# Per-column maxima sent to DRAM as rows, fewer transfers, another PSUM pool for the next keys and values, and a quad every 15.5 units in a planned attention-and-mixer kernel

## The chip, the cores and the metric

One core of a Trainium2 chip runs the whole program; the metric is the device time of one execution in microseconds (us). The engines named here are TensorE (PE, with its weight loads as PEld), VectorE (DVE), ScalarE (ACT), GpSimd (POOL) and SyncE (SP). Transfers are issued by SP, a few by ACT, and each of the two has a queue of its own that takes its instructions in order; 16 DMA engines carry the data.

## The reference

For each of 8 batches and 8 heads there are 576 positions, 64 channels and 32 memory slots. The softmax of `phi` runs over the positions, and so needs the maximum of each of the 32 columns; the sums it weights are the memory's keys and values. Queries attend to these 32 slots, and the result goes through a mixer over tokens and one over channels.

```python
a = np.exp(phi - np.max(phi, axis=2, keepdims=True))      # over the 576 positions
a = a / (np.sum(a, axis=2, keepdims=True) + 1e-09)
k_m = np.einsum('bhsm,bhsd->bhmd', a, k);  v_m = np.einsum('bhsm,bhsd->bhmd', a, v)
scores = scale * np.matmul(q, k_m.transpose(0, 1, 3, 2))
attn = softmax(scores)                                    # over the 32 slots
x = np.matmul(attn, v_m)                                  # then (batch, position, head*channel)
u = x + (np.maximum(x^T @ w_tok1, 0) @ w_tok2)^T          # token mixer
out = u + np.maximum(u @ w_ch1, 0) @ w_ch2                # channel mixer, d_ch = 1536
```

## The kernel before

Work comes in two kinds. A **quad** (b, Q) is four heads of one batch: 16 in all. A **chunk** c is 512 rows of the channel mixer: 9 in all. The program has three stages. In the first, weights are unpacked, the quads (0,0) to (1,1) run, and chunk 0's products start. In the second, which is the one that the change touches, the twelve quads (2,0) to (7,1) of the list `late` run beside chunks 1 and 2. In the third, chunks 3 to 8 run in pairs, with fewer products (their operands are sums of quarters).

The order of all instructions of the second stage is laid down ahead of time by `plan` (line 961): a list scheduler with a duration for each step, one timeline for each engine, a rank for each step (`PERIOD * n` spaces the ranks of the quads), and rooms (buffers) that a step takes. It yields one list; each engine then runs its part of that list strictly in order, with semaphores where data or buffers ask for them. The planner's durations set the order alone. On the chip an instruction that waits holds up all behind it on its engine.

A late quad goes so: `load_turned` (616) brings phi of four heads, one (head, column) on each partition; `phi_max` (620) reduces each partition to one number on DVE; `max_out` (624) writes these 128 numbers to 512 bytes of DRAM, one four-byte word from each partition; `max_in` (628) reads the 512 bytes back to all 128 partitions. POOL subtracts them from phi in its other layout (631), ACT takes the exponential (444), and PE forms keys and values in one PSUM bank `kvp` (`get_kv`, 450). Then come `scales`, `spread_T`, `turn_T`, `get_kb` for the keys and `spread_v`, `v_high`, `v_low` for the values; `scores` (490); the softmax on DVE and ACT, with `ul` (195) and the like between; `rows_out` (544) and `rows_in` (680) turn the result by way of DRAM in pieces of 128 bytes; `nat`, `A`, `R`, `attend` and `u` are the token mixer. A chunk's products `cp` (146) are evicted by ACT (`hh`, 115) and DVE (`hl`, 118) and go into `acc` (169). PSUM has two banks with the tag `at`, two with `ch` and four accumulators; in this kernel every bank of a quad is an `at`, and `ch` belongs to the chunks.

`Sums` writes to DRAM, beside all this, the weight sums that stage three reads back (`load_unit`); `store_u` puts a quad's result in DRAM for the chunks 3 to 8.

Of the kernel before, what the change touches and what calls it, by code (L numbers as in the profile page):

```python
# [10 lines left out]
F32 = mybir.dt.float32  # L11
# [4 lines left out]
ALU = mybir.AluOpType  # L16
AX = mybir.AxisListType
# [3 lines left out]
P = 128  # L21
# [7 lines left out]
def kernel(  # L29
# [312 lines left out]
    class Sums:  # L342
# [5 lines left out]

        def unit(s, j):
            return s.to[:, j].rearrange("p (o x a n) -> p o x a n", o=2, x=2, a=2)  # L350

        def words(s):
# [54 lines left out]
    def load_unit(eng=nc.scalar):  # L407
        if not unit_queue:
            return
        z, p, j = unit_queue.pop(0)  # L410
        t = sb.tile([P, 1024], F32R, tag="c1", name=f"unit{z}{p}{j}", bufs=NF)
        units[z, p, j] = t.rearrange("p (o x a n) -> p o x a n", o=2, x=2, a=2)
        m = 512 if j == 3 else 1024
        eng.dma_start(out=f32(t)[:, :m], in_=sums[p].to[:, j, :m])

# [9 lines left out]
    class Quad:  # L425
# [114 lines left out]
        def rows_out(s):  # L540
            s.rows = dram.tile([S, 4 * M], F32, name="rows" + s.n, tag="rows", bufs=2)
            for i in range(4):
                eng = nc.scalar if i % 2 and (s.b, s.Q) == (4, 0) else nc.sync
                eng.dma_start(
                    out=s.rows[:, i * M : (i + 1) * M].rearrange("(a t) m -> t a m", t=32),
                    in_=s.S[32 * i : 32 * i + 32],
                )
# [60 lines left out]
    class LateQuad(Quad):  # L608


        def __init__(s, b, Q):
            s.b, s.Q, s.n, s.up = b, Q, f"_{b}_{Q}", {}

        def load_turned(s):
# [25 lines left out]
        def get_kv(s):  # L640
            s.step_kv()

# [4 lines left out]

        def vb_room(s):
            s.vb = side[0][:, 640:896]

        def spread_v(s):
            s.vb_room()
# [109 lines left out]

        def spill(s, db):
# [196 lines left out]

    def plan(rank, ways, slow=None, slack=0.0):

# [8 lines left out]
        needs = {z: len(z.after) for z in steps}  # L971
        free, taken, landed, port = {}, {}, 0.0, 0.0
# [26 lines left out]
        while left:  # L999
# [32 lines left out]
    LATE = 2  # L1032
    MARGIN = 0.85
    RANKS = (
# [567 lines left out]
    class ThirdBatchQuad(SecondQuad):  # L1602
# [6 lines left out]

        def spread_v(s):  # L1610
            LateQuad.vb_room(s)
            s.spread_values(s.vb, s.kvp[:, D : 2 * D])

        def get_kv(s):
            s.kvp = bank([P, CW], "kvp" + s.n)
            s.mm_kv()
# [174 lines left out]
    def room(tag, n=1):  # L1791
        return Room((tag, n))
# [15 lines left out]
    def todo_at(t, *args, **kw):  # L1808
        z = step(*args, **kw)
        key[z] = -t  # L1810
        return z
# [36 lines left out]
    u_done = []  # L1848
    PERIOD, START, behind = 12.0, 3.0, []
    for n, qd in enumerate(late):  # L1850
        t0 = START + PERIOD * n

        def do(t, *args, **kw):
            return todo_at(t0 + t, *args, **kw)

        bk, kb, vh, vl, vb, T = room("at", 2), room("kb"), room("vh", 2), room("vl", 2), room("side vb"), room("vb") if n else room("pr", 2)
        per = room("ps", 3)
        if n:
            phi_room, kv_r, q_r = room("phi", 2), room("kv"), room("qT")
            m, r, turned = room("ps", 3), room("pr", 2), room("al", 2)  # L1860
# [4 lines left out]
            z = do(-26, "SP", 0.8, qd.load_phi, begin, take=[phi_room], move=0.9)  # L1865
            y = do(-22, "SP", 0.5, qd.max_in, y, z, take=[r])
            z = do(-16, *PHI_SUB(qd), y, z, use=[phi_room, r], port=True)
            e = do(-13, "ACT", 0.8, qd.phi_only_exp, z, use=[phi_room])
            l = do(-20, "SP", 0.5, qd.load_kv, begin, take=[kv_r], move=3.5)
            lq = do(-12, "SP", 0.6, qd.load_q, begin, take=[q_r], move=1.6)  # L1870
            kvuse, after = [phi_room, kv_r], [e, l]
        else:
            kvuse, after, q_r, lq = [pt2, kv2], [begin], q2, begin
# [4 lines left out]
        else:  # L1878
            y = do(-8, "DVE", 0.35, qd.spread_T, z, take=[T], use=[bk])
        v = do(-7, "DVE", 0.48, qd.spread_v, z, y, sided, take=[vb], use=[bk, side_room, per])  # L1880
        y = do(-7, "PE", 0.12, qd.turn_T, y, use=[bk, T])
        y = do(-6, "ACT", 0.3, qd.get_kb, y, v, take=[kb], use=[bk])
        v = vhigh = do(-5, "ACT", 0.42, qd.v_high, v, take=[vh], use=[vb, side_room])
# [34 lines left out]
        for hf in range(2):  # L1918
# [5 lines left out]
            for db, bk in enumerate(bks):  # L1924
# [14 lines left out]
                wrote[db].append(h)  # L1939
        for db in range(2):  # L1940
            if qd.spill(db):
                z_ = do(25 + db, "SP", 0.5 * len(qd.spill(db)), lambda qd=qd, db=db: qd.store_u(db), *wrote[db], use=[stage[db], side_room], move=0.8)
                z_.lands = True
                u_done.append((qd, z_))

# [52 lines left out]
    for p, x in enumerate(sums):  # L1998
        t0 = SUMS_AT[p]
        w = room("wide", 5)  # L2000
        z = todo_at(t0, "SP", 2.6, x.store_rest, begin, use=c1_rooms[p], move=1.0)
        z.not_before = t0
# [15 lines left out]
            190 + 40 * t, "SP", 0.5, lambda t=t: pr.load(t),  # L2018
            *(z for qd, z in u_done if any(c == pr.c + t for db in range(2) for c, _, _ in qd.spill(db))),
            added[1, NKK - 1], take=[uv[t]], move=2.9,  # L2020
# [427 lines left out]
```

## Time and profile before

| What | Value |
|---|---|
| Runs shown | 784.11, 794.3 and 1462.78 us, median 794.3 us |
| The profiled execution | 790.09 us, span 788.0 us from first to last instruction |
| TensorE granted clock, mean over the span | 0.969 |
| PE busy | 733.8 us, 93% |
| PEld, DVE, ACT, POOL busy | 76%, 64%, 44%, 11% |
| DMA | 101239 packets, 41024 of them under 512 bytes; 196 GB/s over the span |

The profile cuts the span into 40 slices of 19.7 us and gives the busy share of each engine in tenths. Below it names groups of instructions with their mean duration, the idle time ahead of them and what ended it, the transfers with the time from issue to landing, and the chain of work that ended last. The clock granted to TensorE stands beside PE: 1.00 is 2.4 GHz, 0.50 is 1.2 GHz.

### The profile page before, as it was taken

To read this page: it belongs to the slowest core of one execution; us is meant where nothing else is said; L and a number is where in the kernel's file an instruction comes from. 1 tells how busy PE (TensorE), PEld (TensorE's weight loads), DVE (VectorE), ACT (ScalarE), POOL (GpSimd) and SP (SyncE) were. 2 spreads that over 40 slices of the span, in tenths; PEclk is the share of its full clock that TensorE was granted. 3 is DMA by queue.
4 is the path that set the end of the run, shared out by engine and by line. 5 is a ranking of instruction groups with operands and counts; after the bars stand their busy time and mean duration, and the time that the engine had idled before them with its cause. 6 is when DMAs were issued, how large, how long until landed. Compare 5 with 4: busy or idle time off the path is not lost.

```text
span 788.0 us, 11573 instructions
## 1 busy us (share of the span) xinstructions
PE 733.8 (93%) x4371; PEld 596.1 (76%) x4371; DVE 505.2 (64%) x830; ACT 348.6 (44%) x627; POOL 89.7 (11%) x82
## 2 busy tenths in 40 slices
PE   8999999548669999999999998999999999999998
PEld 7778887436547778777887787888778888778887
DVE  4999845435445659564679653897624897524883
ACT  5999662112124343343354343543435543435540
POOL 2122323101011123111040000000000000000000
PEclk9999999769779999999999999999999999999999
DMA  9964626779886889998252785717457626557502
GB/s 361 396 234 149 199 95 164 92 154 200 129 229 181 253 266 290 308 289 247 82 166 92 264 294 191 258 33 274 137 188 245 220 74 232 163 193 249 184 27 80
DMA packets 101239, 155.26 MB, mean 197 GB/s; under 512 B 41024, under 2 KB 67648, under 8 KB 96832
## 3 DMA queue, kind: packets, MB, share of 16 engines
q1 hardware_dynamic: 89488, 121.22, 49.9%
q10 hardware_dynamic: 11696, 33.31, 13.4%
q8 instruction: 34, 0.56, 0.3%
q14 instruction: 21, 0.17, 0.1%
HBM read 117.34 MB, written 37.16 MB: 196 GB/s over the span
## 4 chain that ended last, share of the span: by engine, by line
PE 62%; DMA 24%; DVE 4%; SPq 4%; ACT 2%; issue 2%; POOL 1%; ACTq 0%; POOLq 0%; DVEq 0%
PE ma L292 10%; PE mU L2232 9%; PE cp L146 7%; PE acc L169 7%; PE mB L2232 6%; PE mc L292 5%; DMA kv<-in_kv_dram 5%; DMA phiT<-in_phi_turned_dram 4%; DMA unit<-sums 4%; DMA rows<-S 4%; PE mA L2232 3%; DMA side<-rows 3%; PE mD L2232 3%; PE u L745 2%; PE Ap L565 2%
## 5 line engine op out<-in xcount | busy, mean ns | idle before, releaser
L169 PE MATMUL acc<-hh,c 128*128 128x512 f32 x288 | 103.1, 405 | 0.0
L169 PEld LDWEIGHTS acc<-hh,c 128*128 128x128 f32 x288 | 55.0, 191 | 16.3 <-issue 5.2
L169 PE MATMUL acc<-hl,c 128*128 128x512 f32 x144 | 57.0, 396 | 0.0
L146 PE MATMUL cp<-uh,c1h 128*128 128x512 f32 x144 | 54.8, 421 | 0.0
L146 PE MATMUL cp<-ul,c1h 128*128 128x512 f32 x144 | 51.8, 400 | 0.0
L146 PE MATMUL cp<-uh,c1l 128*128 128x512 f32 x144 | 51.6, 399 | 0.0
L2218 ACT CAST rT<-hid 128x512 fp32r<-128x512 f32 x54 | 32.0, 621 | 26.8 <-PE mB L2232 15.6
L2086 DVE TENSOR_TENSOR hid<-mb,hid 128x512 f32<-128x512 f32 x12 | 8.3, 692 | 50.4 <-ACT hid L2166 50.4
L2219 DVE TENSOR_TENSOR rT<-hid,rT 128x512 fp32r<-128x512 f32 x54 | 35.8, 687 | 7.0 <-ACT rT L2218 7.0
L118 DVE SCALAR_TENSOR_TENSOR hl<-cp,hh 128x512 fp32r<-128x512 f32 x36 | 24.6, 685 | 21.8 <-ACT hh L115 21.7
L695 POOL TENSOR_TENSOR nat<-side,nat 128x512 fp32r<-128x512 f32 (+1 forms) x24 | 22.7, 946 | 117.2 <-ACT nat L687 96.8
L146 PEld LDWEIGHTS cp<-uh,c1h 128*128 128x128 f32 x144 | 27.5, 195 | 8.6 <-issue 4.3
L115 ACT ACTIVATE hh<-cp 128x512 fp32r<-128x512 f32 x36 | 21.6, 600 | 26.7 <-PE cp L146 26.6
L146 PEld LDWEIGHTS cp<-uh,c1l 128*128 128x128 f32 x144 | 27.9, 194 | 6.4
L450 PE MATMUL kvp<-kv,phi 128*32 128x130 f32 x440 | 16.6, 302 | 16.5 <-DMA kv<-in_kv_dram 10.4
L146 PEld LDWEIGHTS cp<-ul,c1h 128*128 128x128 f32 x144 | 28.1, 195 | 4.6
L292 PE MATMUL ma<-xrest_p,unit 128*128 128x512 f32 x108 | 28.1, 396 | 3.7 <-DMA unit<-sums 3.6
L745 PE MATMUL u<-w2h,Rh 128*128 128x288 f32 x96 | 31.5, 328 | 0.0
L2089 ACT ACTIVATE hid<-hid 128x512 f32<-128x512 f32 x24 | 15.2, 632 | 36.3 <-DVE hid L2086 32.1
L169 PEld LDWEIGHTS acc<-hl,c 128*128 128x128 f32 x144 | 27.7, 192 | 4.3
L565 PE MATMUL Ap<-w1h,nat 128*128 128x256 f32 x126 | 25.3, 293 | 5.7 <-DVE ul L195 5.7
L631 POOL TENSOR_TENSOR phi<-phi,prr 128x640 f32<-128x640 f32 x11 | 17.1, 1551 | 118.6 <-DMA prr<-top 112.3
(373 smaller groups left out, 1929.0 us busy)
## 6 DMA issues: line engine op xcount, KB each, us to landing
unit<-sums ACTq DMA_DIRECT2D x54, 512.0 KB, 5.1
kv<-in_kv_dram SPq DMA_DIRECT2D x12, 1300.0 KB, 7.3
rawc<-in_w_ch_dram SPq DMA_DIRECT2D x12, 1024.0 KB, 7.9
q<-in_q_dram SPq DMA_DIRECT2D x16, 576.0 KB, 8.6
sums<-sums SPq DMA_DIRECT2D x12, 512.0 KB, 8.8
u_p<-spilled SPq DMA_DIRECT2D x6, 1024.0 KB, 8.0
phi<-in_phi_dram SPq DMA_DIRECT2D x16, 320.0 KB, 7.3
unit<-sums ACTq DMA_DIRECT2D x18, 256.0 KB, 3.6
```

The source lines that it names most:

```text
L115: nc.scalar.activation(out=h, in_=ps, func=AF.Relu)
L118: nc.vector.scalar_tensor_tensor(out=l, in0=ps, scalar=0.0, in1=f32(h), op0=ALU.max, op1=ALU.subtract)
L146: nc.tensor.matmul(ps, l[:, a, w], r[:, a], start=n == 0, stop=n == len(mm) - 1)
L169: nc.tensor.matmul(ps, l_[f // 2][:, f % 2, a * P : (a + 1) * P], r[:, w], start=f == start and x == 0, stop=f == end - 1 and x == 2,)
L292: nc.tensor.matmul(ps, l, r, start=first and n == 0, stop=n == len(mm) - 1, skip_group_check=not first,)
L565: nc.tensor.matmul(ps[:, :TT], a, w, start=x == 0, stop=x == len(mm) - 1)
L631: eng.tensor_tensor(out=s.pt, in0=s.pt, in1=s.r.rearrange("p (i m) -> p i m", i=4) .unsqueeze(2) .to_broadcast([P, 4, NC, M]), op=ALU.subt ...
L695: eng.tensor_tensor(out=o, in0=a, in1=f32(h), op=ALU.subtract)
L745: nc.tensor.matmul(s.up[db, hf][:, :HALF], a, r, start=False, stop=x == len(mm) - 1)
L2218: nc.scalar.copy(out=t[:, 0], in_=x)
L2219: nc.vector.tensor_tensor(out=t[:, 1], in0=x, in1=f32(t[:, 0]), op=ALU.subtract)
L2232: nc.tensor.matmul(s.banks[room][a][:, w], l_[:, a * P : a * P + P], r_, start=not (p or x) and name in ("11", "T1", "21", "T4"), stop=p = ...
```

## The change

- **Maxima as rows.** `phi_max` reduces into the first column of the tile that it read, and then a DVE transposition in blocks of 32x32 puts the 32 maxima of each head into one row. `max_out` sends four rows of 128 bytes in place of 128 words of 4. The tile `m` is gone.
- **Fewer transfers.** `store_rest` issues 4 transfers for each `Sums` in place of 6 (the order of the pieces in DRAM changes, and `load_unit` reads by that order), `store_u` one for both halves of a quad in place of two. Quad (4,0) issues its `rows_out` all from SP.
- **Rooms.** `kvp` of the twelve late quads moves from the tag `at` to `ch`. The copy of the keys `T` takes the room of `kb`; the spread values `vb` have two rooms, one in `side` and one of their own.
- **The planner.** The quads' ranks are 15.5 apart, and `scores` of a quad isn't placed ahead of its turn. `load_turned` stands behind the scores of three quads before. A load counts as landed later (2.5 in place of 0.85, with 8.0 for the turned phi and 6.0 for `rows_in`), each queue's landings apart, and SP's steps get the slack that only PE's had.

```diff
         def store_rest(s):
             for x in range(2):
                 h = f32(c1[s.p][x])
-                for o in range(2):
-                    nc.sync.dma_start(out=s.unit(0)[:, o, x], in_=h[:, 2 * o : 2 * o + 2, :P])
-                nc.sync.dma_start(out=s.unit(3)[:, 0, x], in_=h[:, 2:, P:])
+                for j, src in ((0, h[:, :, :P]), (3, h[:, 2:, P:])):
+                    n = src.shape[1] * P
+                    to = s.to[:, j, x * n : x * n + n].rearrange("p (a n) -> p a n", n=P)
+                    nc.sync.dma_start(out=to, in_=src)
...
         def phi_max(s):
-            s.m = wp.tile([P, 1], F32, tag="ps", name="m" + s.n, bufs=3)
-            nc.vector.tensor_reduce(out=s.m, in_=s.turned, axis=AX.X, op=ALU.max)
+            t = s.turned
+            nc.vector.tensor_reduce(out=t[:, :1], in_=t, axis=AX.X, op=ALU.max)
+            nc.vector.transpose(out=t[:, M : 2 * M], in_=t[:, :M])
 
         def max_out(s):
             s.top = dram.tile([1, 4 * M], F32, name="top" + s.n, tag="maxima", bufs=2)
-            nc.sync.dma_start(out=s.top.rearrange("a n -> n a"), in_=s.m)
+            nc.sync.dma_start(
+                out=s.top.rearrange("a (i m) -> (a i) m", m=M), in_=s.turned[:: P // 4, M : 2 * M]
+            )
...
         def get_kv(s):
-            s.step_kv()
+            s.step_kv(pch.tile([P, CW], F32, tag="ch", name="kvp" + s.n, bufs=2))
...
-        def vb_room(s):
-            s.vb = side[0][:, 640:896]
+        def vb_room(s, room):
+            s.vb = side[0][:, 640:896] if room.tag[0] == "s" else sb.tile([P, 256], F32, tag="vb", name="vb" + s.n, bufs=1)
...
-            s.T = sb.tile([P, 2, D], F32, tag="vb", name="T" + s.n, bufs=1)
+            s.T = sb.tile([P, 2, D], F32, tag="kb", name="T" + s.n, bufs=1)
...
-        def store_u(s, db):
-            for c, lo, hi in s.spill(db):
-                o = 896 + S * db - S * s.b
+        def store_u(s):
+            v = side[0][:, 896:].rearrange("p (a n) -> p a n", a=2)
+            for c, lo, hi in s.spill():
                 nc.sync.dma_start(
-                    out=spilled[c][:, 2 * s.Q + db, lo - CW * c : hi - CW * c], in_=side[0][:, o + lo : o + hi]
+                    out=spilled[c][:, 2 * s.Q : 2 * s.Q + 2, lo - CW * c : hi - CW * c],
+                    in_=v[:, :, lo - S * s.b : hi - S * s.b],
                 )
...
-                t = max(t, y.end if y.eng == z.eng and not y.lands else y.ready + slack * (z.eng == "PE"))
+                t = max(t, y.end if y.eng == z.eng and not (y.lands or y.move and y.eng == "ACT") else y.ready + slack * (z.eng in ("PE", "SP")))
...
-            if eng == "SP":
-                landed = max(landed, z.begin + 2.2) + 0.91 * z.move + 1.6 * (z is slow)
-                z.ready = max(landed + MARGIN, z.end + z.tail)
+            if eng == "SP" or z.move:
+                landed[eng] = max(landed.get(eng, 0.0), z.begin + 2.2) + 0.91 * z.move + 1.6 * (z is slow)
+                z.ready = max(landed[eng] + margin, z.end + z.tail)
...
-    PERIOD, START, behind = 12.0, 3.0, []
+    PERIOD, START, behind, scored, vlows = 15.5, 3.0, [], [begin], []
...
-            y = do(-32, "SP", 0.5, qd.load_turned, begin, take=[turned], move=0.9)
-            y = do(-27, "DVE", 0.72, qd.phi_max, y, take=[m], use=[turned])
-            y = do(-26, "SP", 0.5, qd.max_out, y, use=[m])
+            y = do(-32, "SP", 0.45, qd.load_turned, scored[max(n - 2, 0)], take=[turned], move=0.8)
+            y.tail = 8.0 if n > 1 else 4.0
+            y = do(-27, "DVE", 0.85, qd.phi_max, y, use=[turned])
+            y = do(-26, "SP", 0.45, qd.max_out, y, use=[turned], move=0.01)
...
         z = do(0, "PE", 1.05, qd.scores, y, lq, take=[*ss, S_], use=[q_r, kb])
-        former = [z, vlow]
+        z.not_before = t0
+        former, vlows = [z, *vlows[-1:]], vlows + [vlow]
+        scored.append(z)
...
         z = do(9, "SP", 1.0, qd.rows_in, z, sided, take=[raw], use=[side_room], move=0.8)
+        z.tail = 6.0
...
-    order = plan(key, dict.fromkeys(steps, 0), None, SLACK)
+    order = plan(key, dict.fromkeys(steps, 0), None, SLACK, 2.5)
```

What the planner makes of this is read from the order of the built program. A row is a line, an operation, and the tile written and read; a name ends in the batch, the half Q and a running number. The first place is SP's queue from where quad (2,1)'s rows are read back (`rows_in`, written to `side`). Before:

```order
L680 DMA side_1422<-rows_2_1_1787 128x4x128
L683 DMA side_1422<-rows_2_1_1787 64x128
L616 DMA phiT_6_0_1864<-in_phi_turned_dram 128x576
L544 DMA rows_3_0_1892<-S_3_0_1824 32x18x32 x4
L624 DMA top_5_1_1922<-m_5_1_1898 128x1
L624 DMA top_6_0_1934<-m_6_0_1912 128x1
L616 DMA phiT_6_1_1938<-in_phi_turned_dram 128x576
L616 DMA phiT_7_0_1948<-in_phi_turned_dram 128x576
L773 DMA spilled3_104<-side_1422 128x192
L680 DMA side_1422<-rows_3_0_1892 128x4x128
```

The same region of SP's queue in the change, from `max_in` of quad (3,1) to that of quad (4,0):

```order
L644 DMA prr_3_1_1692<-top_3_1_1631 128x128
L629 DMA phiT_4_0_1699<-in_phi_turned_dram 128x576
L380 DMA sums0_1379<-sums0_1591 128x1024 x2
L621 DMA kv_3_1_1765<-in_kv_dram 128x2600
L617 DMA phi_4_0_1770<-in_phi_dram 128x640
L545 DMA rows_2_1_1807<-S_2_1_1694 32x18x32 x4
L638 DMA top_4_0_1829<-phiT_4_0_1699 4x32
L696 DMA side_1422<-rows_2_1_1807 128x4x128
L699 DMA side_1422<-rows_2_1_1807 64x128
L644 DMA prr_4_0_1891<-top_4_0_1829 128x128
```

Before, while quad (2,1)'s rows go in, the queue holds the maxima of (5,1) and (6,0) and the turned phi of (6,0) to (7,0); in the change it holds those of (4,0) alone, three quads on.

The second place is DVE's queue about the first eviction `ul` of quad (2,0)'s result (`u00_2_0`, `u10_2_0`; these free the PSUM banks that `attend` takes next). Before:

```order
L118 SCALAR_TENSOR_TENSOR hl5_1_1875<-cp5_1_1838,hh5_1_1874 128x512
L620 TENSOR_REDUCE m_5_1_1898<-phiT_5_1_1809 128x1
L195 TENSOR_TENSOR ul_2_1386<-u00_2_0_1866,uh_2_1385 128x288
L195 TENSOR_TENSOR ul_2_1386<-u10_2_0_1867,uh_2_1385 128x288
L620 TENSOR_REDUCE m_6_0_1912<-phiT_6_0_1864 128x1
L479 TENSOR_TENSOR vl_3_0_1950<-side_1422,vh_3_0_1932 128x256
L195 TENSOR_TENSOR ul_2_1386<-u01_2_0_1914,uh_2_1385 128x96
```

The same evictions in the change:

```order
L633 TENSOR_REDUCE phiT_4_0_1699<-phiT_4_0_1699 128x1
L634 STREAM_TRANSPOSE phiT_4_0_1699<-phiT_4_0_1699 128x32
L118 SCALAR_TENSOR_TENSOR Rl_2_0_1820<-Rp_2_0_1791,Rh_2_0_1805 128x512
L118 SCALAR_TENSOR_TENSOR hl5_1_1823<-cp5_1_1778,hh5_1_1822 128x512
L195 TENSOR_TENSOR ul_2_1386<-u00_2_0_1831,uh_2_1385 128x288
L195 TENSOR_TENSOR ul_2_1386<-u10_2_0_1832,uh_2_1385 128x288
L481 TENSOR_TENSOR vl_3_0_1881<-side_1422,vh_3_0_1877 128x256
L719 TENSOR_TENSOR al_2_1_1893<-aT_2_1_1803,ah_2_1_1879 128x576
L195 TENSOR_TENSOR ul_2_1386<-u01_2_0_1861,uh_2_1385 128x96
```

Before, the reduction of (5,1)'s phi stands right ahead of the two evictions and that of (6,0) right behind; in the change it is that of (4,0), four rows earlier, with its transposition, and none stands between the evictions and the rest of the quad.

## Rows read from the trace of the kernel before

**Rows 1.** The page's 40 slices: busy tenths of PE.

```profile
PE   8999999548669999999999998999999999999998
```

**Rows 2.** Two stretches: length, then busy time of each engine, clock, DMA share, GB/s.

```profile
140.00:240.00 100.00, 63.60 (x417) 48.97 (x416) 44.26 (x84) 21.89 (x47) 12.96 (x11) 0.78 0.83 157
240.00:430.00 190.00, 184.86 (x1409) 147.53 (x1408) 127.52 (x228) 75.40 (x160) 38.29 (x32) 1.00 0.72 224
```

**Rows 3.** Waits of PE from 140 to 240: us in total, times, longest.

```profile
PE kvp L450 <- DMA kv<-in_kv_dram: 10.4, 1, 10.4
PE u L736 <- DVE ul L195: 8.4, 1, 8.4
PE kvp L450 <- ACT phi L444: 6.1, 1, 6.1
PE Ap L565 <- DVE ul L195: 5.7, 1, 5.7
PE sp L490 <- ACT kb L664: 3.2, 1, 3.2
PE kvp L660 <- DVE side L1129: 2.5, 1, 2.5
```

**Rows 4.** The six busy stretches of PE behind these waits: the third, and the sum.

```profile
173.90:179.40 5.50, 5.50 (x48) 4.44 (x49) 2.98 (x7) 1.77 (x4) 3.28 (x3) 0.50 0.84 231
...
sum 23.90, PE 23.90 PEld 19.34 DVE 14.88 ACT 6.18 POOL 5.17; mean PE 3.98 PEld 3.22 DVE 2.48 ACT 1.03 POOL 0.86
```

**Rows 5.** Waits of DVE from 140 to 240.

```profile
DVE m L620 <- DMA phiT<-in_phi_turned_dram: 29.8, 6, 9.3
```

**Rows 6.** The transfers of the maxima by their tile: ns to issue, first and last start.

```profile
L624 SPq DMA_DIRECT2D top<-m x11: 319/383/1837, 129.3 to 232.4; - x11
```

**Rows 7.** Two stretches, columns as in rows 2.

```profile
234.00:238.00 4.00, 4.00 (x16) 3.43 (x15) 2.29 (x5) 0.46 (x2) 0.00 (x0) 0.55 0.04 9
...
152.00:164.00 12.00, 8.94 (x44) 5.82 (x43) 9.48 (x20) 3.10 (x6) 1.53 (x1) 0.85 0.85 50
```

**Rows 8.** The transfers of 232.3 to 232.5, the last of the eleven.

```profile
top<-m SPq DMA_DIRECT2D x1, 0.5 KB, 7.6
```

**Rows 9.** Transfers by line: count, KB each, median us from issue to landing.

```profile
kv<-in_kv_dram SPq DMA_DIRECT2D x12, 1300.0 KB, 7.3
...
rows<-S SPq DMA_DIRECT2D x54, 72.0 KB, 3.3
...
top<-m SPq DMA_DIRECT2D x11, 0.5 KB, 9.9
```

**Rows 10.** Groups of instructions from 123 to 430: busy us, mean ns, idle before.

```profile
L631 POOL TENSOR_TENSOR phi<-phi,prr 128x640 f32<-128x640 f32 x11 | 17.1, 1551 | 118.6 <-DMA prr<-top 112.3 <-DMA rows<-S 6.2
...
L118 DVE SCALAR_TENSOR_TENSOR hl<-cp,hh 128x512 fp32r<-128x512 f32 x24 | 16.4, 684 | 16.9 <-ACT hh L115 16.8
L115 ACT ACTIVATE hh<-cp 128x512 fp32r<-128x512 f32 x24 | 14.3, 596 | 21.9 <-PE cp L146 21.9
...
L674 DVE STREAM_TRANSPOSE S<-sp 128x288 f32<-128x288 f32 x24 | 10.5, 464 | 8.7 <-PE sp L490 8.6
...
L620 DVE TENSOR_REDUCE m<-phiT 128x1 f32<-128x576 f32 x11 | 8.2, 746 | 31.5 <-DMA phiT<-in_phi_turned_dram 31.5
...
L444 ACT ACTIVATE phi<-phi 128x640 f32<-128x640 f32 x11 | 8.1, 738 | 18.2 <-POOL phi L631 18.2
```

**Rows 11.** Landing of the turned phi, by its tile.

```profile
DMA to landing us min/median/max: 5.2/10.5/14.2
```

**Rows 12.** Landing of the maxima read back, by the tile `prr`.

```profile
DMA to landing us min/median/max: 5.2/7.4/11.3
```

**Rows 13.** The chain that ended last: start us, us, what.

```profile
304.95 2.72 PE cp L146 x12
...
372.99 1.66 PE Ap L565 x14
374.66 1.25 PE kvp L450 x40
```

More of the change, by code (lines that the diff above doesn't have):

```diff
@@ L411, in load_unit @@
         t = sb.tile([P, 1024], F32R, tag="c1", name=f"unit{z}{p}{j}", bufs=NF)
-        units[z, p, j] = t.rearrange("p (o x a n) -> p o x a n", o=2, x=2, a=2)
         m = 512 if j == 3 else 1024
+        v = t[:, :m]
+        units[z, p, j] = (
+            v.rearrange("p (o x a n) -> p o x a n", x=2, a=2, n=P) if j in (1, 2)
+            else v.rearrange("p (x o a n) -> p o x a n", x=2, a=2, n=P)
+        )
         eng.dma_start(out=f32(t)[:, :m], in_=sums[p].to[:, j, :m])
@@ L612, in __init__, with load_phi, load_kv, load_q @@
             s.b, s.Q, s.n, s.up = b, Q, f"_{b}_{Q}", {}
+        def load_phi(s):
+            s.pt = sb.tile([P, 4, NC, M], F32, tag="phi", name="phi" + s.n, bufs=2)
+            nc.sync.dma_start(out=s.pt, in_=phi[s.b, s.Q])
+        def load_kv(s):
+            s.kv = kv_room("kv" + s.n)
+            nc.sync.dma_start(out=s.kv, in_=kv[s.b, s.Q])
+        def load_q(s):
+            s.qT = sb.tile([P, 4, HALF], F32, tag="qT", name="q" + s.n, bufs=1)
+            nc.sync.dma_start(out=s.qT.rearrange("p i n -> p (i n)"), in_=q[s.b, s.Q])
         def load_turned(s):
@@ L761, in u_low, with spill @@
             mixer(WIN - 1).put_low(2 * s.Q + db, to, s.up[db, hf][:, :n])
-        def spill(s, db):
+        def spill(s):
             return [
@@ L959, with plan @@
     OVERLAP = {"ACT": 0.09, "DVE": 0.07}
-    def plan(rank, ways, slow=None, slack=0.0):
+    def plan(rank, ways, slow=None, slack=0.0, margin=0.85):
         then = {z: [] for z in steps}
@@ L971, in plan @@
         needs = {z: len(z.after) for z in steps}
-        free, taken, landed, port = {}, {}, 0.0, 0.0
+        free, taken, landed, port = {}, {}, {}, 0.0
         left, done = [z for z in steps if not z.after], []
@@ L1608, with spread_v @@
             locals()[name] = vars(LateQuad)[name]
-        def spread_v(s):
-            LateQuad.vb_room(s)
+        def spread_v(s, room):
+            LateQuad.vb_room(s, room)
             s.spread_values(s.vb, s.kvp[:, D : 2 * D])
         def get_kv(s):
-            s.kvp = bank([P, CW], "kvp" + s.n)
+            s.kvp = pch.tile([P, CW], F32, tag="ch", name="kvp" + s.n, bufs=2)
             s.mm_kv()
@@ L1854, in do @@
             return todo_at(t0 + t, *args, **kw)
-        bk, kb, vh, vl, vb, T = room("at", 2), room("kb"), room("vh", 2), room("vl", 2), room("side vb"), room("vb") if n else room("pr", 2)
+        bk, kb, vh, vl, vb, T = room("ch", 2), room("kb"), room("vh", 2), room("vl", 2), Room(("side vb", 1), ("vb", 1)), room("kb") if n else room("pr", 2)
         per = room("ps", 3)
@@ L1859 @@
             phi_room, kv_r, q_r = room("phi", 2), room("kv"), room("qT")
-            m, r, turned = room("ps", 3), room("pr", 2), room("al", 2)
-            y = do(-32, "SP", 0.5, qd.load_turned, begin, take=[turned], move=0.9)
-            y = do(-27, "DVE", 0.72, qd.phi_max, y, take=[m], use=[turned])
-            y = do(-26, "SP", 0.5, qd.max_out, y, use=[m])
+            r, turned = room("pr", 2), room("al", 2)
+            y = do(-32, "SP", 0.45, qd.load_turned, scored[max(n - 2, 0)], take=[turned], move=0.8)
+            y.tail = 8.0 if n > 1 else 4.0
+            y = do(-27, "DVE", 0.85, qd.phi_max, y, use=[turned])
+            y = do(-26, "SP", 0.45, qd.max_out, y, use=[turned], move=0.01)
             y.lands, y.tail = True, 2.4
-            z = do(-26, "SP", 0.8, qd.load_phi, begin, take=[phi_room], move=0.9)
-            y = do(-22, "SP", 0.5, qd.max_in, y, z, take=[r])
+            z = do(-26, "SP", 0.45, qd.load_phi, begin, take=[phi_room], move=0.9)
+            y = do(-22, "SP", 0.45, qd.max_in, y, z, take=[r], move=0.1)
             z = do(-16, *PHI_SUB(qd), y, z, use=[phi_room, r], port=True)
             e = do(-13, "ACT", 0.8, qd.phi_only_exp, z, use=[phi_room])
-            l = do(-20, "SP", 0.5, qd.load_kv, begin, take=[kv_r], move=3.5)
-            lq = do(-12, "SP", 0.6, qd.load_q, begin, take=[q_r], move=1.6)
+            l = do(-20, "SP", 0.45, qd.load_kv, begin, take=[kv_r], move=3.5)
+            lq = do(-12, "SP", 0.45, qd.load_q, begin, take=[q_r], move=1.6)
             kvuse, after = [phi_room, kv_r], [e, l]
@@ L1879 @@
             y = do(-8, "DVE", 0.35, qd.spread_T, z, take=[T], use=[bk])
-        v = do(-7, "DVE", 0.48, qd.spread_v, z, y, sided, take=[vb], use=[bk, side_room, per])
-        y = do(-7, "PE", 0.12, qd.turn_T, y, use=[bk, T])
-        y = do(-6, "ACT", 0.3, qd.get_kb, y, v, take=[kb], use=[bk])
+        v = do(-8, "DVE", 0.48, lambda qd=qd, r=vb: qd.spread_v(r), *([z] if n else [z, y]), sided, take=[vb], use=[bk, side_room, per])
+        y = do(-7, "PE", 0.12, qd.turn_T, y, v, use=[bk, T])
+        y = do(-6, "ACT", 0.3, qd.get_kb, y, take=[kb], use=[bk])
         v = vhigh = do(-5, "ACT", 0.42, qd.v_high, v, take=[vh], use=[vb, side_room])
@@ L1939 @@
                 wrote[db].append(h)
[L1940 to L1944, printed above, removed]
+        if qd.spill():
+            z_ = do(25.5, "SP", 0.5 * len(qd.spill()), qd.store_u, *wrote[0], *wrote[1], use=[*stage, side_room], move=1.6)
+            z_.lands = True
+            u_done.append((qd, z_))
     chain = []
@@ L2000 @@
         w = room("wide", 5)
-        z = todo_at(t0, "SP", 2.6, x.store_rest, begin, use=c1_rooms[p], move=1.0)
+        z = todo_at(t0, "SP", 1.8, x.store_rest, begin, use=c1_rooms[p], move=1.0)
         z.not_before = t0
@@ L2018 @@
             190 + 40 * t, "SP", 0.5, lambda t=t: pr.load(t),
-            *(z for qd, z in u_done if any(c == pr.c + t for db in range(2) for c, _, _ in qd.spill(db))),
+            *(z for qd, z in u_done if any(c == pr.c + t for c, _, _ in qd.spill())),
             added[1, NKK - 1], take=[uv[t]], move=2.9,
```

11 lines of the change are left out of this document (4 added, 7 removed).

## The prediction

> **What bounds the kernel now.** I read the slices first [rows 1]. PE shows 8 or 9 tenths nearly everywhere, and falls to 4 to 6 in four slices between 138 and 236 us. That is the second stage, the one that the change plans anew. The table of two stretches puts numbers to it [rows 2]: from 140 to 240 PE is busy 63.6 of 100 us, from 240 to 430 it is busy 184.9 of 190, and the mean granted clock is 0.78 in the one and 1.00 in the other. So the same kind of work loses a third of its time in the first stretch and 2.7% in the second.
>
> The waits name what ended the idle times [rows 3]. Six waits make 36.3 us of the 36.4 idle ones: for a load of keys and values (10.4), for the exponential of phi (6.1), for DVE's eviction `ul` (8.4 and 5.7), and for `kb` and the spread values (3.2 and 2.5). Behind each, PE runs for a while at a granted clock of 0.50, the 1.2 GHz level: six stretches of 23.9 us in all [rows 4], in which it does the work of 12.0 us at 2.4 GHz. The loss is 36.4 + 12.0 = 48.4 us.
>
> Two of these waits are not what they are called. `ul` is short; on DVE's queue it stands behind reductions of phi that wait for their load, 29.8 us in the stretch [rows 5]. The order shows the pair: the reduction of quad (5,1) right ahead of the first evictions of (2,0). PE waits for a bank that DVE can't free, since DVE waits for phi of a quad that comes seven places later.
>
> Why are those loads late? The DMA share is 0.83 in the bad stretch at 157 GB/s and 0.72 in the good one at 224 [rows 2]: busy, and moving less. All eleven `max_out` fall between 129.3 and 232.4 us, and none later [rows 6]. The last one is alone: from 234 to 238 the DMA engines move 9 GB/s [rows 7], and yet its 512 bytes take 7.6 us to land [rows 8]; the median of the eleven is 9.9 [rows 9]. While these transfers are out, other loads crawl: from 152 to 164 the engines are 0.85 busy at 50 GB/s [rows 7]. `rows_out` issues 72 KB in pieces of 128 bytes, 576 pieces, and lands in 3.3 us [rows 9]. So it is the single words that are dear, and small pieces as such are not.
>
> **The change, part by part.**
>
> Maxima as rows. Eleven transfers of 128 words become eleven of four 128-byte pieces. No row has this transfer; the nearest is `rows_out` with its pieces of the same size, 3.3 us. The bounds are 3.3 below (it has many more pieces, so I give nothing below it) and 9.9 above, if it is no better than the words. I take 3.3. What then goes is the crawl of the other loads in the bad stretch, and with it the waits of PE for keys and values and for the exponential, 16.5 us of [rows 3].
>
> The Trainium skill (DMA: Bandwidth & Descriptors, Specifications) says that transfers in pieces under 512 bytes are done as read-modify-write; by this rule 128-byte rows are of the words' kind, and their price might stay. The 3.3 us of [rows 9] for 576 such pieces against 7.6 us of [rows 8] for 128 words speak against it. By the rule the sum would be that of the first rival below.
>
> New on DVE is a transposition of 128x32. The nearest row is the one of 128x288 at 0.46 us [rows 10]; between nothing and that, eleven make at most 5.1 us, on an engine busy 44 of 100 and 128 of 190 us [rows 2]. It ends no wait of PE as long as DVE has that idle time; if the cover were gone it would cost those 5.1 us. I count nothing.
>
> The planner's order. `load_turned` now waits in the plan for the scores of three quads before, so the reduction that stands at the evictions of (2,0) is four quads on, not seven. It stands four rows ahead of them with other work between, and none follows right behind. That takes the 14.1 us of waits for `ul` out, and the two smaller ones, which stand behind ACT and DVE work that is late for the same loads. PE's work is the same list of products.
>
> Without waits, the low clock has no cause, and the 12.0 us go as well. What was 51.6 us of work (100 - 48.4) then runs like the later stretch, which keeps 2.7% idle: 1.4 us stay. Gain 47.0 us.
>
> What is late next. The maxima now come just in time, all through the stage. The chain of a quad is: turned phi 10.5, reduction 0.75, transposition at most 0.46, rows out 3.3, read back 7.4, subtraction 1.55, exponential 0.74, in all 24.7 us [rows 9 to 12]. For the room it has, take (4,0): its turned phi is issued just behind the `max_in` of (3,1). From there to (3,1)'s keys and values go 7.4 + 1.55 + 0.74 = 9.7 us, and between the two `kvp` PE's order has the first one itself (1.25), twelve pieces of three chunk products (a fourth of 2.72 each, 8.2) and one `A` (1.66) [rows 13], 11.1 in all: 20.8 us. The chain is 3.9 us short, if PE stands right behind; if it has 4 us of lead, nothing. For the eight quads whose chains now run in the later part that is 0 to 31 us. I take 3, near the low end, since the row for a well-fed stage [rows 2] shows PE as the bound, with work queued ahead of each step, and so with lead.
>
> Keys and values in `ch`. `kvp` no longer competes with `A`, `R`, scores and `u` for the two `at`, and takes one of the two banks of the chunk for as long as its keys and values are read. The cost lies between nothing and one full eviction for each late quad that a chunk product waits for, 0.60 + 0.68 = 1.28 us [rows 10], twelve times 15.4 us. The cover is the `acc` products that stand between two `cp` on PE, 2.7 us; I count nothing and keep 15.4 for the range.
>
> Fewer transfers: 12 issues less in `store_rest`, 20 in `store_u`, two moved from ACT to SP. The bytes are the same. None of the waits in [rows 3] ends with either; the order of SP's queue is a part of the term above. The second room of the spread values takes away a wait between two quads, of which the 2.5 us in [rows 3] are the most that PE saw; they are in the 36.4.
>
> **The sum.** The profiled execution took 790.1 us; 790.1 - 47.0 + 3 = 746.1. The runs shown have 784.1 and, as their median, 794.3: the profiled one lies between these, within 0.8% of either.
>
> **Rivals.**
>
> *The rows cost what the words cost.* Then the loads crawl as before, only spread over the stage, and the gain is what the order alone brings: the 14.1 us of `ul` and its share of the low clock, 14.1/36.3 of 12.0, so 4.7, together 18.8 and 771 us. If the crawl then also meets the later stretch, nothing is left, and 790. For it: no row has a transfer of four pieces. Against: [rows 9], as read above. Chance 0.13.
>
> *The maxima come too late, and the kernel is slower.* Place: PE at `kvp` of the eight late quads. With the slowest landings seen, 14.2 and 11.3 in place of 10.5 and 7.4 [rows 11, 12], the chain is 3.9 + 3.7 = 7.6 us short (the slower read back lengthens both sides alike), 61 us over eight quads, and each such wait is followed by a stretch at 0.50, as in [rows 4], at half of 4 us: 16 more. 790.1 - 47.0 + 77 = 820. It decides when the shortage passes 47.0 / 8 = 5.9 us a quad; over 2% slower needs 7.9 with the low clock in it. For it: before, after the last maximum, PE runs undisturbed to 430, and in the change that stretch has the chains in it. Against: the largest landings come from the crawl that goes. Chance 0.07.
>
> *The chunk lacks its bank, or the chain is short in part.* 15.4 us or half of the 31: 790.1 - 47.0 + 15.4 = 758.5, with a few us either way. For it: one `ch` bank is left at times, and ACT, which frees it, has waits of its own. Chance 0.17.
>
> **How the numbers follow.** The forecast, 735 to 757 us, has 0.60; it is the likeliest, and 746 is its time. Below 735, where the later stretch would lose its 5.1 idle us as well (790.1 - 48.4 - 5.1 = 736.6), I put 0.03. The third rival, 757 to 770, has 0.17; the first, 0.13, lies from 766 to 790, a quarter of it below 770; the second 0.07, most of it above 806. A range of 735 to 770 holds 0.60 + 0.17 + 0.03 = 0.80. About 2% can be told from no change: below 774.3 is faster, above 805.9 slower. Faster: 0.03 + 0.60 + 0.17 + 0.05 = 0.85. Slower: 0.05 of the second rival. The rest, 0.10, is within 2%.
>
> **What would show it.** In the profile after, the transfer from `phiT` to `top` should land in 3 to 4 us, with no stretch in the second stage of DMA over 0.8 at 50 GB/s; DVE's wait for the turned phi should fall from 29.8 to some us; PE should be at 9 tenths from 140 to the end with the clock at 1.00, and the third stage begin some 45 us earlier. If `top` still takes 8 us, the first rival holds. If PE waits at `kvp` for the exponential, quad after quad, it is the second; at `cp` for `hl`, the third. A slower first or third stage, or loads of weight sums that come late because the second stage is short, would make the prediction wrong in a way that I have not priced.

## The result, and the profile after

The changed kernel takes 740.12 us, median of four runs (738.27 to 742.34), against 790.05 for the kernel before in the same series, the median of 784.11, 785.8, 794.3 and 1462.78: 50 us less. The last of these was disturbed and is left out of the ratio, 0.939 (95% interval 0.931 to 0.948); against the mean of the other three, 788.1, it is 48 us. The forecast was 746.1 in a range of 735 to 770. The profiled execution took 739.23 us, with a span of 737.4 and a mean granted clock of 0.999.

The page's slices of the changed kernel, PE, its granted clock and the DMA share in tenths, answer to [rows 1]:

```profile
PE   8999999999999999899997999999999999999998
PEclk9999999999999999999999999999999999999999
DMA  9965632787979999962436877065559154668302
```

The hole of four slices is gone, and no slice is under 9 tenths of the full clock. The two stretches, columns as in [rows 2], with the second one cut at 380, where the third stage now begins:

```profile
140.00:240.00 100.00, 99.59 (x832) 78.67 (x834) 77.41 (x144) 39.79 (x88) 23.38 (x17) 1.00 0.85 258
240.00:380.00 140.00, 133.18 (x998) 107.58 (x987) 97.70 (x170) 58.25 (x118) 31.85 (x26) 1.00 0.70 224
```

The DMA share from 140 to 240 is what it was (0.83 before), and at that share the engines now carry 258 GB/s in place of 157. So the engines counted as busy before without moving much; which pieces took so long is counted under the experiments. The first `mb`, which opens the third stage, starts at 379.4 us in place of 429.5.

PE's longest waits from 124 to 400 (us in total, times, longest), and DVE's only wait for the turned phi there, beside 29.8 us in [rows 5]:

```profile
PE mc L292 <- DMA unit<-sums: 3.9, 2, 2.1
PE kvp L452 <- ACT phi L446: 3.3, 2, 1.8
PE u L752 <- DVE Rl L118: 2.2, 1, 2.2
```

```profile
DVE phiT L633 <- DMA phiT<-in_phi_turned_dram: 0.4, 1, 0.4
```

The landings of the turned phi and then of the maxima read back, by their tiles (before: [rows 11, 12]), and the line of `rows_out` from the list of transfers (before: 3.3 in [rows 9]):

```profile
DMA to landing us min/median/max: 2.8/6.0/11.3
...
DMA to landing us min/median/max: 3.4/4.1/7.3
```

```profile
rows<-S SPq DMA_DIRECT2D x56, 72.0 KB, 2.1
```

The transfer of the rows itself has no landing in the trace, so the 3 to 4 us that the prediction named as its sign can't be read. A bound is SP's queue, here by start and length of each issue: the rows of one quad are issued at 136.25, and the `prr` that reads them, the second one behind them, 4.6 us later.

```profile
136.25 0.52 SPq L638 DMA_DIRECT2D top<-phiT  x1
...
140.87 0.47 SPq L644 DMA_DIRECT2D prr<-top  x1
```

Of the 50.6 us that the span lost, 34.8 are idle time of PE (788.0 - 733.8 = 54.2 before, 737.4 - 718.0 = 19.4 after), and 15.8 are PE's busy time: the same 4371 products, at a mean granted clock of 0.999 in place of 0.969.

### The profile page after: what moved, and what is told of

Its sections match the earlier page's. It is cut to its first block, busy times and chain, and to the rows that moved or that the text cites. A ratio compares the mean times of both kernels' runs of the same rounds, so it can differ in the third digit from the quotient of the medians.

```text
span 737.4 us, 11507 instructions
## 1 busy us (share of the span) xinstructions
PE 718.0 (97%) x4371; PEld 585.7 (79%) x4371; DVE 512.5 (70%) x841; ACT 349.8 (47%) x627; POOL 93.6 (13%) x82
## 4 chain that ended last, share of the span: by engine, by line
PE 63%; DMA 9%; DVE 8%; issue 1%; ACT 1%; POOL 1%; SPq 0%; DVEq 0%; POOLq 0%
PE ma L292 10%; PE mU L2251 10%; PE mB L2251 7%; PE acc L169 6%; PE cp L146 6%; DMA unit<-sums 5%; PE mc L292 5%; PE u L761 4%; PE mD L2251 3%; PE mA L2251 3%; PE Ap L566 2%; PE mb L292 2%; PE u L752 1%; DMA phi<-in_phi_dram 1%; PE kvp L452 1%
## 5 line engine op out<-in xcount | busy, mean ns | idle before, releaser
L169 PE MATMUL acc<-hh,c 128*128 128x512 f32 x288 | 100.0, 396 | 0.0
L146 PE MATMUL cp<-uh,c1h 128*128 128x512 f32 x144 | 52.9, 408 | 0.0
L2237 ACT CAST rT<-hid 128x512 fp32r<-128x512 f32 x54 | 32.0, 621 | 26.8 <-PE mB L2251 15.6
L711 POOL TENSOR_TENSOR nat<-side,nat 128x512 fp32r<-128x512 f32 (+1 forms) x24 | 24.6, 1026 | 105.7 <-ACT nat L703 99.4
L2237 ACT CAST r<-hid 128x512 fp32r<-128x512 f32 x36 | 22.4, 623 | 14.2 <-PE mU L2251 5.4
L292 PE MATMUL mc<-xw2h_p,unit 128*128 128x512 f32 x72 | 24.6, 395 | 4.5 <-DMA unit<-sums 4.5
L647 POOL TENSOR_TENSOR phi<-phi,prr 128x640 f32<-128x640 f32 x11 | 18.7, 1704 | 80.2 <-DMA prr<-top 33.5
```

The source lines that it names most:

```text
L146: nc.tensor.matmul(ps, l[:, a, w], r[:, a], start=n == 0, stop=n == len(mm) - 1)
L169: nc.tensor.matmul(ps, l_[f // 2][:, f % 2, a * P : (a + 1) * P], r[:, w], start=f == start and x == 0, stop=f == end - 1 and x == 2,)
L292: nc.tensor.matmul(ps, l, r, start=first and n == 0, stop=n == len(mm) - 1, skip_group_check=not first,)
L647: eng.tensor_tensor(out=s.pt, in0=s.pt, in1=s.r.rearrange("p (i m) -> p i m", i=4) .unsqueeze(2) .to_broadcast([P, 4, NC, M]), op=ALU.subt ...
L711: eng.tensor_tensor(out=o, in0=a, in1=f32(h), op=ALU.subtract)
L2237: nc.scalar.copy(out=t[:, 0], in_=x)
```

## The experiments

The theory behind the prediction (W): the 128 single words of each `max_out` slow the loads that run beside them, and all else follows. Its rival (O): the planner's order did it, which put reductions of quads far ahead in front of evictions. The first two runs part the two.

**Words in the new order.** The changed kernel, with `max_out` as before; the reduction and transposition stay.

```diff
-                out=s.top.rearrange("a (i m) -> (a i) m", m=M), in_=s.turned[:: P // 4, M : 2 * M]
+                out=s.top.rearrange("a n -> n a"), in_=s.turned[:, :1]
```

> The changed kernel with one thing undone: the reduction and the transposition stay, but the maxima go out as 128 words of 4 bytes from 128 partitions, as in the kernel before. The order of all engines is that of the changed kernel. If the words slow the other loads (theory W), the loss comes back, now spread over the stage: 771 to 790 us, the turned phi and the maxima read back land 2 us or more later than in the changed kernel (6.0 and 4.1 us), and the clock falls below 1.00 at places. If it was the order that held PE up, reductions far ahead of their quad (theory O), the words cost only their own longer landing: 738 to 748 us, with the clock at 1.00.

Measured: 795.27 us, ratio to the kernel before 1.008 (1.004 to 1.011). PE, ACT, DVE and POOL execute the changed kernel's list in its order, row for row. The two stretches, PE's longest wait from 140 to 380, and the landing of the words, the maxima read back, the turned phi and the keys and values:

```profile
140.00:240.00 100.00, 85.57 (x660) 67.55 (x659) 57.35 (x114) 30.80 (x69) 15.75 (x13) 0.91 0.86 197
240.00:380.00 140.00, 111.83 (x855) 89.42 (x854) 76.14 (x138) 42.98 (x94) 25.25 (x22) 0.89 0.92 231
```

```profile
PE kvp L452 <- ACT phi L446: 15.6, 3, 7.2
```

```profile
top<-phiT SPq DMA_DIRECT2D x11, 0.5 KB, 11.1
prr<-top SPq DMA_DIRECT2D x11, 64.0 KB, 4.9
phiT<-in_phi_turned_dram SPq DMA_DIRECT2D x11, 288.0 KB, 5.8
kv<-in_kv_dram SPq DMA_DIRECT2D x12, 1300.0 KB, 13.3
```

The whole gain is gone, and the time is 5 us over what W allowed for; the loss is spread over the stage with the words. One sign of W did not come: the turned phi lands no later than in the change (5.8 against 6.0 us at the median) and the maxima read back only 0.8 us later. The loads that land late in this order are others, keys and values above all (13.3 against 7.1). O is wrong: its order without the rows is no better than the old one.

**Rows in the old order.** The kernel before, with the transposition and the rows alone.

```diff
-            s.m = wp.tile([P, 1], F32, tag="ps", name="m" + s.n, bufs=3)
-            nc.vector.tensor_reduce(out=s.m, in_=s.turned, axis=AX.X, op=ALU.max)
+            t = s.turned
+            s.m = wp.tile([P, M], F32, tag="mrow", name="m" + s.n, bufs=2)
+            nc.vector.tensor_reduce(out=t[:, :1], in_=t, axis=AX.X, op=ALU.max)
+            nc.vector.transpose(out=s.m, in_=t[:, :M])
...
-            nc.sync.dma_start(out=s.top.rearrange("a n -> n a"), in_=s.m)
+            nc.sync.dma_start(out=s.top.rearrange("a (i m) -> (a i) m", m=M), in_=s.m[:: P // 4])
```

> The kernel before with one thing done: the maxima are transposed on DVE and go out as four rows of 128 bytes. The planner, its ranks, rooms and all other transfers are those of the kernel before, so the reduction of quad (5,1) still stands right ahead of the evictions of (2,0). Theory W: the loads no longer crawl, DVE's wait for the turned phi falls from 29.8 us to under 8, and 740 to 752 us. Theory O: DVE still stands at reductions of quads far ahead, 771 to 790 us.

Measured: 747.19 us, ratio 0.948 (0.942 to 0.953). The rows bring 42.8 us of the 50 by themselves (790.01, the kernel before in this series, less 747.19). PE's waits for `ul` and DVE's for the turned phi from 140 to 240:

```profile
PE u L738 <- DVE ul L195: 2.3, 1, 2.3
PE Ap L565 <- DVE ul L195: 2.2, 1, 2.2
```

```profile
DVE phiT L621 <- DMA phiT<-in_phi_turned_dram: 6.4, 2, 3.3
```

The order of PE, ACT and POOL is that of the kernel before. The waits for `ul` fell from 14.1 [rows 3] to 4.5 us in the same order, and beside them DVE's wait for the turned phi from 29.8 [rows 5] to 6.4.

**What makes a word dear.** Five runs add a second transfer to the changed kernel, behind each of the eleven `max_out`: words of 4 bytes from the same tile to DRAM that nobody reads. They differ in where the words land.

```diff
+            s.more = dram.tile([1, 4 * M], F32, name="more" + s.n, tag="more", bufs=2)
+            nc.sync.dma_start(out=s.more.rearrange("a n -> n a"), in_=s.turned[:, :1])
...
+            s.more = dram.tile([P, 4 * M], F32, name="more" + s.n, tag="more", bufs=2)
+            nc.sync.dma_start(out=s.more[:, :1], in_=s.turned[:, :1])
```

The first pair writes them side by side, the second 512 bytes apart. For 64 and 16 bytes apart the tile is `[P, M // 2]` and `[P, M // 8]`; for 32 words it is `[1, M]`, read from `s.turned[:M, :1]`.

> The changed kernel with eleven more transfers, one behind each transfer of the maxima: 128 words of 4 bytes from 128 partitions into 512 bytes of DRAM that nobody reads. Nothing waits for them but the room of the turned phi. Theory W: 760 to 790 us, since the words slow whatever load stands behind them. Theory O: 738 to 746 us.

> As the run with more words, but each of the 128 extra words goes to a line of its own, 512 bytes from the next. If a word is dear because 128 of them are written into the same 512 bytes (theory L), this costs little: within 4 us of the changed kernel, 738 to 744 us, and lands in 3 to 4 us. If it is the piece of 4 bytes as such (theory P), it costs what the dense words cost, within a third of that loss.

> As the run with more words apart, but each word 64 bytes from the next, so that eight stand in 512 bytes and none in the same 64. The dense words cost 54 us more than those 512 bytes apart. If words collide only within 64 bytes or less: within 4 us of the words far apart, 740 to 746 us. If they collide within 512 bytes: eight to a line in place of 128, so between, 746 to 785 us.

> As the runs with more words apart, with each word 16 bytes from the next: four stand in 64 bytes, 32 in 512. Words 64 and 512 bytes apart cost nothing (741 and 742 us), 128 words side by side 54 us. If words collide when they share 64 bytes: 755 to 796 us. If they collide only in a smaller piece: 738 to 746 us.

> The changed kernel with eleven more transfers of 32 words of 4 bytes from 32 partitions into 128 contiguous bytes that nobody reads. If the cost goes by the word: a fourth of the 54 us of 128 dense words, 752 to 757 us. If it goes by the square of the words that meet in a line: a sixteenth, 742 to 746 us. If it goes by the transfer: 780 us or more.

| Words beside the rows | us | ratio to the kernel before (95%) |
|---|---|---|
| none (the change, measured again) | 741.61 | 0.937 (0.933 to 0.942) |
| 128, 512 bytes apart | 742.33 | 0.941 (0.935 to 0.947) |
| 128, 64 bytes apart | 741.45 | 0.945 (0.938 to 0.951) |
| 128, 16 bytes apart | 744.29 | 0.947 (0.943 to 0.951) |
| 32, side by side | 759.29 | 0.967 (0.957 to 0.977) |
| 128, side by side | 796.29 | 1.010 (1.007 to 1.013) |

The number of packets on the page is the same for all four kinds of 128 words, 100782. Side by side they cost 54.7 us (796.29 - 741.61), 5.0 for each transfer, and 6 us more than W allowed for. 16 bytes apart or more they cost 0 to 2.7 us by these times; the kernel before differs by some us between the series, and by the ratios it is some 3, 6 and 7 us for 512, 64 and 16 bytes, of which only the last lies outside the interval of the change measured again. The same two stretches with the words side by side, and 512 bytes apart:

```profile
284.00:296.00 12.00, 8.41 (x70) 5.81 (x74) 8.36 (x14) 1.83 (x3) 5.66 (x4) 0.72 1.03 168
158.00:164.00 6.00, 6.00 (x41) 4.27 (x40) 3.38 (x6) 2.53 (x5) 1.29 (x1) 1.00 0.93 57
```

```profile
284.00:296.00 12.00, 10.76 (x97) 8.16 (x96) 8.98 (x17) 4.37 (x8) 3.25 (x3) 1.00 1.02 311
158.00:164.00 6.00, 6.00 (x70) 5.08 (x69) 3.63 (x9) 1.81 (x5) 1.59 (x1) 1.00 0.91 317
```

Both kernels run the same list of products, though at a given time the first is further back in it. At the same share it is 57 against 317 GB/s and 168 against 311. These are short stretches with words in them; from 128 to 350 us it is 218 against 256 GB/s, at shares of 0.95 and 0.83.

The trace has a time for each piece that the DMA engines moved. From 124 to 440 us, the pieces that took more than 2 us, none of them a word, number 134 in the kernel before (80 of these are pieces of the turned phi) and 1 in the change. With words beside the rows there are 244 for 128 side by side, 96 for 32 side by side, and 17, 9 and 3 for 128 at 16, 64 and 512 bytes apart. So the words hold up some pieces of other transfers, and these are few and long: the median piece of the turned phi takes 93 ns in all of these runs.

So it isn't the number of words as such, nor their size, but that they are written next to each other. That bears out theory L in its direction and not in its size: words that share 64 bytes, four at 16 bytes, collide little, if at all. With 32 words the loss is 17.7 us, a third of the 54.7 for a fourth of the words, and 2 us over the range that was set for a cost by the word: roughly by the word, and neither by its square nor by the transfer.

**The rest of the change.** Between the rows in the old order (747.2) and the change (740.1 and 741.6) lie 6 to 7 us. Three runs undo one part each, with the change measured beside them: the place of `kvp` (and with it the planner's room), the late load of the turned phi, the spacing.

```diff
-        bk, kb, vh, vl, vb, T = room("ch", 2), room("kb"), room("vh", 2), room("vl", 2), Room(("side vb", 1), ("vb", 1)), room("kb") if n else room("pr", 2)
+        bk, kb, vh, vl, vb, T = room("at", 2), room("kb"), room("vh", 2), room("vl", 2), Room(("side vb", 1), ("vb", 1)), room("kb") if n else room("pr", 2)
...
-            s.step_kv(pch.tile([P, CW], F32, tag="ch", name="kvp" + s.n, bufs=2))
+            s.step_kv()
...
-            y = do(-32, "SP", 0.45, qd.load_turned, scored[max(n - 2, 0)], take=[turned], move=0.8)
+            y = do(-32, "SP", 0.45, qd.load_turned, begin, take=[turned], move=0.8)
...
-    PERIOD, START, behind, scored, vlows = 15.5, 3.0, [], [begin], []
+    PERIOD, START, behind, scored, vlows = 12.0, 3.0, [], [begin], []
...
-        z.not_before = t0
```

> The changed kernel itself, beside the three that follow, so that few us can be told. All theories: 738 to 742 us.

> The changed kernel with one thing undone: the keys and values of the late quads go to a bank of the tag at again, and the planner orders the steps by that. If the bank's place is worth nothing, as the prediction counted it: within 2 us of the change. If the at banks are what the quads run short of (theory B): 745 to 750 us, with PE waiting for evictions ul, Rl or S. If chunks lose more by lending ch: 735 to 738 us.

> The changed kernel with one thing undone: the turned phi is loaded as early as its buffers allow, not behind the scores of three quads before. If the just-in-time chain of the maxima costs what PE still waits at kvp for the exponential (3.3 us): 736 to 739 us. If the early reductions hold up DVE as before, even with rows: 744 to 749 us, as the old order with rows (747). If neither matters: within 2 us of the change.

> The changed kernel with the spacing undone: ranks of the quads 12.0 apart, and scores not held back to their turn. If the spacing is what gains the 7 us between the old order with rows (747) and the change (740): 745 to 748 us, with quads crowded ahead of 240 us and PE idle there. If it was the loads' due times or the rooms: within 2 us of the change.

Measured: 741.61 for the change; 760.99 with `kvp` in `at`, ratio 0.963 (0.958 to 0.968); **734.25 with the early phi, ratio 0.929 (0.925 to 0.933)**; 742.47 with the quads 12 apart, ratio 0.940 (0.935 to 0.945).

The spacing is worth nothing that can be told. The fewer transfers, the rooms of `T` and `vb` and the planner's later landings were not undone by themselves, so what each is worth stays open. The bank is worth 19 us, more than either theory of that run had, and in the other direction from the cost that the prediction allowed for. To see by what, one more run gives the bank to the old plan, with the rows:

```diff
-        bk, kb, vh, vl, vb, T = room("at", 2), room("kb"), room("vh", 2), room("vl", 2), room("side vb"), room("vb") if n else room("pr", 2)
+        bk, kb, vh, vl, vb, T = room("ch", 2), room("kb"), room("vh", 2), room("vl", 2), room("side vb"), room("vb") if n else room("pr", 2)
...
-            s.step_kv()
+            s.step_kv(pch.tile([P, CW], F32, tag="ch", name="kvp" + s.n, bufs=2))
```

> The kernel before with two things done: rows for the maxima, and the late quads' keys and values in a ch bank; the planner's rules, ranks and other rooms are those of the kernel before. Rows alone gave 747 us there, and the new plan loses 20 us when the keys and values go back to at. If the bank is what the quads lack under any plan: 742 us or less, most of the way to the change (740). If it is needed only by the new plan, where it was made for it: 745 to 750 us. If lending a chunk's bank costs chunks: over 750 us.

Measured: 756.54 us, ratio 0.964 (0.960 to 0.967), 9 us more than the rows in the old plan without it, as the third guess had it. But that guess, that lending costs the chunks, doesn't say why one and the same bank gains 19 us in one plan and loses 9 in the other. The order gives one. This counts, on PE's list, how many of the 432 products `cp` (chunks 0 to 2) stand ahead of the last quad's `kvp`, and ahead of the last `u`:

```
                          last kvp   last u   median us
change (ch)                 360        432      741.6
change, kvp in at           414        432      761.0
old plan with rows (at)     369        420      747.2
old plan with rows and ch   336        387      756.5
```

With `at` in the new plan the quads fall behind the chunks. The last `kvp` and the last `u` of that kernel start at 358.4 and 409.7 us, those of the change at 315.1 and 377.6; first that kernel, then the change:

```profile
L452 PE MATMUL kvp<-kv,phi x440: 271/273/298, 152.7 to 358.4; 128*32 128x130 f32 x147
L761 PE MATMUL u<-w2h,Rh x96: 290/296/607, 171.7 to 409.7; 128*128 128x288 f32 x96
```

```profile
L452 PE MATMUL kvp<-kv,phi x440: 271/273/298, 146.1 to 315.1; 128*32 128x130 f32 x147
L761 PE MATMUL u<-w2h,Rh x96: 290/296/403, 164.8 to 377.6; 128*128 128x288 f32 x96
```

The last `cp` of the kernel with `at` starts at 365.5, and in the 44 us behind it PE has, but for twelve `acc`, only the quads' chains to run. The stretch, and PE's two longest waits from 320 to 410:

```profile
366.00:410.00 44.00, 32.75 (x195) 27.23 (x180) 22.94 (x36) 16.84 (x33) 3.45 (x4) 0.84 0.31 97
```

```profile
PE Rp L572 <- ACT Ah L727: 5.7, 2, 5.3
PE u L752 <- DVE Al L731: 4.4, 2, 3.8
```

In these 44 us 11.3 are idle and the mean clock is 0.84; this plan has its hole at the end of the stage. (The profiled execution took 767.58 us, 6.6 over the median of this run.) No run keeps the change's order and moves the bank alone, so the bank and the order that is made with it are not told apart. In the old plan with `ch` it is the other way round: the last `u` is done with 45 `cp` left over. That one's loss I have not followed to its waits, so for it the counts are a reading and not a proof.

The early phi beats both kernels, the change by 7.4 us, and is 2 us under the least that was expected. It was expected to save the waits of PE at `kvp` for the exponential, and they are gone: 3.3 us in the change's first profile, 0.8 in its second, none here. But the gain is mostly elsewhere. The first `mb` starts at 378.2 us, against 379.4 and 378.7 in the two profiles of the change, so at most 1.2 us are gained ahead of it; from there to the end it is 353.6 us against 358.0. The chain of the changed kernel at the start of the third stage, a step of ACT ahead of that chain, and 390 to 400 us in the change and with the early phi:

```profile
387.94 0.33 ACT hidal L2108
388.28 0.09 issue
388.37 10.25 DMA unit<-sums
398.62 0.14 issue
398.75 1.39 PE mc L292 x5
```

```profile
383.80 1.05 ACT L318 CAST ch<-cw 128x1024 fp32r<-128x1024 f32 x1 [3.17 <-DVE cw L317]
```

```profile
390.00:400.00 10.00, 6.09 (x27) 4.41 (x26) 3.18 (x5) 3.12 (x5) 0.00 (x0) 1.00 0.91 318
```

```profile
390.00:400.00 10.00, 10.00 (x45) 8.22 (x45) 7.83 (x15) 3.80 (x6) 0.00 (x0) 1.00 0.58 188
```

The change waits there for weight sums that ACT issues at 388, behind an activation. PE's list from the first `mb` on is the same in both kernels. But in the change five steps of DVE and one of ACT that prepare sums (`cw`, `ch`) still stand behind that `mb`, and ACT waits 3.2 us for DVE ahead of its one; with the early phi all six are done before it. PE's waits for the sums in the third stage are 1.6 us with the early phi and 5.8 in the change. So an edit in the second stage's plan reached into the third, and most of this gain came by another way than the one that was expected.

## Why the prediction was right, and where it was not

- **Waits and low clock from 140 to 240** (gain 47.0). Right in place and size: 0.4 us stay idle there, where the forecast left 1.4. The clock gave more than its 12.0 us, 15.8 by PE's busy time. I had counted only the busy stretches behind the six waits, 23.9 us; by the mean clock, (1 - 0.969) x 788.0 / 0.5 = 49 us of the span, idle ones among them, stood at the 1.2 GHz level.
- **Which part brings it.** Here a step failed: "That takes the 14.1 us of waits for `ul` out", said of the new order. With the old order and the rows the 14.1 are 4.5; with the new order and the words the kernel is no faster than before. The place of the reduction was where the late load became visible, and not why it was late. I split the gain into some 28 us for the rows and 18.8 for the order; the runs give 42.8 and 6 to 7. The total came out because the change makes both; for either part alone this split would have given a wrong time.
- **First rival, rows at the price of words.** It did not come. Its 771 us for a kernel with the new order and dear transfers were too kind: that kernel takes 795, near the 790 that the prediction gave in case the crawl reached the later stretch too, as it does.
- **Just-in-time maxima** (+3, between 0 and 31). PE's waits for the exponential are 3.3 us in one profile of the change and 0.8 in a second. The second rival's mechanism does exist: with the words in the new order these same waits are 15.6 us, the largest there.
- **`kvp` in `ch`** (nothing, at most 15.4 dearer). Mis-sized, and of the wrong sign: in this plan the bank is worth 19 us. I priced the lending and not what the `at` banks gain, and took the order of the built program as given, although that order was made with this bank.
- **The later stretch.** 240 to 380 loses 6.8 us where 240 to 430 lost 5.1 before; of the 3 us that I allowed, 1.7.
- **Loads of weight sums**, named as not priced. PE waits for them 5.8 us in the third stage, against 5.3 before, so leaving them out cost the forecast nothing that can be told.

Against the profiled execution the forecast was 6.9 us too high: 3.8 from the clock, 2.8 from idle time (34.8 us less, where 36.4 - 1.4 - 3 = 32.0 were forecast), the rest from time outside the span.

## What to carry to other kernels

Look for a stretch where the DMA share is high and the bytes per second are low, and for a transfer there that writes single words next to each other; turn it into rows, or space the words (here only words that nobody reads were spaced), before touching the order. A wait in an in-order queue shows where a late load hurts, and its position is not yet the cause. Where a planner orders the work, price a buffer's move by planning without it, and look whether the two kinds of work still end together; that the second decides is a reading of four plans here, and no run tests it alone.

## What was not expected of the hardware

- 128 words of 4 bytes written side by side cost 5.0 us of the kernel for each transfer, and the same words 16, 64 or 512 bytes apart at most some tenths: (744.29 - 741.61) / 11 = 0.24 us at 16 bytes, and 0.7 by the ratios. They slow what runs beside them, as the 57 GB/s where the other kernel moves 317 and the pieces of over 2 us (244 against 3) show. By what the words hold them up, no run here shows.
- The Trainium skill (DMA: Bandwidth & Descriptors, Specifications) has pieces under 512 bytes done as read-modify-write. All these words are such pieces, and so are the 128-byte rows; the trace doesn't agree that this sets the price, since it is the spacing that does. Why 4 bytes apart is dear and 16 is not, and what lies between, no run here shows.
